# Row numbers of a group written behind the gates of the same group

## The chip, the cores and the metric

The kernel runs on one core of a Trainium2 chip. Its time is the device time of one execution in microseconds, from the first to the last instruction and the little around them. The kernel before was run three times (2207.92, 2194.14 and 2196.41 us, median 2196.41) and once more under the hardware profiler (2205.68 us, of which the span of its instructions is 2203.8 us). In what follows PE is TensorE, DVE is VectorE, ACT is ScalarE, POOL is GpSimd and SP is SyncE; PEld is the loading of weights into TensorE.

## The reference

Two stages follow one another. The first is an attention without softmax, for 8 batches of 2496 tokens with 256 channels; the second sends each of the 19968 resulting rows through one of 8 experts.

```python
scores = z @ z.T / S                       # per batch, z is 2496 x 64
x = u * (maximum(scores, 0) ** 2 @ v)      # 2496 x 256 per batch
logits = normed(x) @ normed(expert_emb).T / tau
e = argmax(logits); gate = softmax(logits)[e]
out = gate * (maximum(x @ w1[e], 0) @ w2[e])   # 256 -> 1024 -> 256
```

## The kernel before

**Attention.** Each batch is cut into five groups of tokens (four of 512, the last of 448) and twenty slices of 128 keys. For a step (batch, group, slice) PE forms the scores of the slice against the group (L266, L267), ACT takes relu and square out of PSUM (L269, L270), DVE splits the result into a high and a low float16 part (L290, L291), and PE multiplies both parts with the split values into the accumulators of the group (L329, L331, L333). Scores are symmetric, so a block above the diagonal is turned by a DMA transpose on SP's queue (L297, L299) instead of being computed again. Steps whose slices were made by an earlier group ask nothing of ACT and DVE; the last group of a batch consists of little else.

**Routing.** When the twenty steps of a group are done, the function `route` deals out its work in nineteen pieces, one per step of the next group: `gate_x` multiplies the accumulators by u (L361, tile xt), `turn` brings the result into token order with PE (L367, L368), `square`, `root` and `scale` give the norm (L374, L617 to L631, L387 to L396), `splits` writes x as two float16 halves into the tile `row` (L404 on ACT, L405 on DVE), `top` picks the expert (L415 to L427, tile ob), `gates` writes the gate weight (L441) and the row number of each token (L443) into the same tile `row`, `rank` counts the tokens of each expert on PE (L450, L451, from ob), `place` makes the target rows (L460 to L468) and `scatters` sends the four pieces of `row` into the DRAM table xs with four indirect DMAs on POOL's queue (L474). POOL clears the end of each row (L444) and the tile ob (L426).

**Slots of row.** The tile `row` comes from a pool with two buffers. So the row of a group takes the buffer of the group two before it, and whoever writes it first waits until the four scatters of that older group have landed.

**Experts.** The rows of xs are read back in tiles and multiplied with the split weights (L878 to L880 up, L902 to L904 down), and each result is scattered to its place in the output (L909). This stage begins about 1360 us into the span.

**What sets the order.** PE's order is the order in which the program is written. DVE, ACT, POOL and, up to the experts, SP are ordered by a scheduler that knows what an instruction reads and writes and has its own estimate of durations. It may put an instruction far ahead of its neighbours in the program when its inputs are there. `tc.issue_after(x)` puts the instructions of its block behind `x` in the order of their engine; it adds no wait. Each engine works through its queue in order: an instruction that waits holds back all that is queued behind it.

The row numbers (L443) read only a constant. In the kernel before, the scheduler puts the L443 of a group into DVE's queue while the group before it is at its `root`, about one group ahead of the rest of its `gates`.

Of the kernel before, what the change touches and what calls it, by code (L numbers as in the profile page):

```python
# [14 lines left out]
ALU = mybir.AluOpType  # L15
# [16 lines left out]
def ceil_div(a, b):  # L32
    return -(-a // b)
# [11 lines left out]
def relu2_attention_then_moe(ctx, tc, zT, uT, v, emb, tau, w1, w2, ident, tri, iota_e, out):  # L45
    nc = tc.nc
    B, D, S = uT.shape
# [293 lines left out]
    def route(b, g, acc, ut):  # L341

        t0, n = groups[g]
        nj = ceil_div(n, P)
        eps, oinv = scan[b, "out"]
# [8 lines left out]
        row = rt.tile([P, 4, ROW], F32, name="row", tag="row")  # L354
        rowi = row.bitcast(I32)
        row16 = row.bitcast(F16)
        loc = {}
# [78 lines left out]
        def gates():  # L436
            sm = rt.tile([P, 4], F32, name="sm", tag="sm")
            nc.vector.tensor_reduce(sm[:, :nj], loc["ex"][:, :nj, :], axis=AX.X, op=ALU.add)
            nc.vector.tensor_scalar_add(sm[:, :nj], sm[:, :nj], 1e-9)
            nc.vector.reciprocal(sm[:, :nj], sm[:, :nj])  # L440
            nc.vector.scalar_tensor_tensor(row[:, :nj, D:D + 1], sm[:, :nj].unsqueeze(2), oinv,  # L441
                                           loc["dn"][:, :nj].unsqueeze(2), op0=ALU.mult, op1=ALU.mult)
            nc.vector.tensor_scalar_add(rowi[:, :nj, D + 1:D + 2], idb[:, :nj].unsqueeze(2), float(b * S + t0))  # L443
            nc.gpsimd.memset(row[:, :, D + 2:], 0.0)  # L444

        def rank():
# [43 lines left out]
        def sq(j):  # L490
# [3 lines left out]
        return [gate_x, lambda: None, turn(0), both(turn(1), take(0)), both(take(1), sq(0)), both(turn(2), sq(1)),  # L494
                both(turn(3), take(2)), both(take(3), sq(2)), sq(3), root, scale, top, exps, splits(0),
                splits(2), gates, rank, place, scatters]


# [473 lines left out]
    for i, (b, g, q, s) in enumerate(steps):  # L972
# [16 lines left out]
        if i == 6:  # L989
# [7 lines left out]
            idb = iot[:, 4 * E:4 * E + 4]  # L997
# [156 lines left out]
```

## Time and profile before

| | |
|---|---|
| three runs | 2194.14, 2196.41, 2207.92 us, median 2196.41 |
| the profiled execution | 2205.68 us, span 2203.8 us |
| PE, PEld | busy 97% and 64% of the span |
| DVE, ACT, POOL | busy 60%, 49%, 16% |
| PE's mean granted clock | 0.991 |
| attention with routing | from about 22 us to about 1360 us |
| experts | about 1360 us to the end |

The profile is read from the top: the busy shares say which engine could be the bound, the table of stretches says in which stage it has idle time left, the lists of waits say who ended that idle time, and the order in time shows one case of it. A matmul's busy time is longer than the distance to the next one, since they overlap in the array: a 128x512 matmul is shown with 0.38 us, and the next one starts 0.22 us later.

### The profile page before, as it was taken

The page shows a single profiled execution, that of the slowest core. Times are in us where ns is not written, and L with a number is a line of the kernel's source. Part 1 is how long each engine was busy: PE and PEld are TensorE (multiplying, and loading weights), DVE is VectorE, ACT ScalarE, POOL GpSimd, SP SyncE. Part 2 cuts the span into 40 slices and gives each one's busy share as a digit, 9 for nine tenths or more (in the row PEclk, how much of TensorE's full clock was granted, in tenths as well). Part 3 has the DMA queues.
Part 4 walks back from the last instruction along what each step waited for, and adds up shares of the span by engine and source line. Part 5 has one row for each costly group of instructions (what it writes and reads, how often), then busy time and mean ns, then how long its engine had stood idle before and what let it go on. Part 6 is the DMA issues. An engine that isn't in the chain of part 4 may idle for free. (4 is left out here: it accounts for less than half of the span.)

```text
span 2203.8 us, 41437 instructions
## 1 busy us (share of the span) xinstructions
PE 2141.8 (97%) x14634; PEld 1409.9 (64%) x14634; DVE 1313.1 (60%) x3821; ACT 1080.1 (49%) x2283; POOL 346.0 (16%) x428
## 2 busy tenths in 40 slices
PE   6999999999999999999999999999999999999999
PEld 2444444445445445454455456888888888888898
DVE  7777777768767877876777755433333333333333
ACT  7667666657648757666757654222222222222221
POOL 0011111111111112111011111221111111111111
PEclk9999999999999999999999999999999999999999
DMA  7958867776866957866765853434233332237485
GB/s 196 210 105 211 171 145 180 164 190 154 201 143 162 212 129 201 164 177 167 153 172 124 178 111 94 119 88 93 68 68 92 92 88 49 57 107 203 122 218 117
DMA packets 552724, 313.85 MB, mean 142 GB/s; under 512 B 475189, under 2 KB 513086, under 8 KB 544320
## 3 DMA queue, kind: packets, MB, share of 16 engines
q1 hardware_dynamic: 537040, 269.53, 53.7%
q0 software_dynamic: 15184, 41.24, 5.9%
q8 instruction: 117, 1.92, 0.4%
q14 instruction: 95, 0.78, 0.1%
q10 hardware_dynamic: 288, 0.39, 0.1%
HBM read 272.94 MB, written 59.60 MB: 151 GB/s over the span
## 5 line engine op out<-in xcount | busy, mean ns | idle before, releaser
L269 ACT ACTIVATE a<-sc 128x512 f32<-128x512 f32 (+1 forms) x480 | 268.2, 559 | 157.0 <-PE sc L267 99.2
L270 ACT ACTIVATE a<-a 128x512 f32<-128x512 f32 (+1 forms) x480 | 286.3, 597 | 11.7
L333 PEld LDWEIGHTS <-vv 128*128 128x128 f16 x1600 | 157.4, 98 | 188.4 <-issue 12.6
L329 PEld LDWEIGHTS <-vv 128*128 128x128 f16 x1600 | 157.2, 98 | 161.6 <-issue 3.8
L331 PEld LDWEIGHTS <-vv 128*128 128x128 f16 x1520 | 149.5, 98 | 168.9 <-issue 20.1
L909 POOL DMA_INDIRECT out_dram<-ot,me x159 | 154.6, 973 | 653.8 <-DVE ot L908 618.8
L904 PE MATMUL po<-w,hl 128*128 128x256 f16 x928 | 253.0, 273 | 0.0
L903 PE MATMUL po<-w,hh 128*128 128x256 f16 x928 | 253.0, 273 | 0.0
L902 PE MATMUL po<-w,hh 128*128 128x256 f16 x928 | 252.9, 273 | 0.0
L474 POOL DMA_INDIRECT xs<-row,dsti x160 | 172.7, 1079 | 419.9 <-DMA xs<-row,dsti 361.9
L329 PE MATMUL acc<-tt,vv 128*128 128x512 f16 (+1 forms) x640 | 236.4, 369 | 0.0
L331 PE MATMUL acc<-tt,vv 128*128 128x512 f16 (+1 forms) x640 | 236.3, 369 | 0.0
L908 DVE TENSOR_SCALAR ot<-po,me,w 128x256 f32<-128x256 f32 x116 | 58.2, 539 | 219.2 <-PE po L904 216.6
L333 PE MATMUL acc<-tt,vv 128*128 128x512 f16 (+1 forms) x640 | 184.0, 369 | 0.0
L266 PE MATMUL sc<-z 128*128 128x512 f16 (+1 forms) x480 | 177.0, 369 | 3.1 <-DVE z L189 3.1
L267 PE MATMUL sc<-z,z 128*128 128x512 f16 (+1 forms) x480 | 177.0, 369 | 0.0
L903 PEld LDWEIGHTS <-hh 128*128 128x128 f16 x1272 | 124.5, 98 | 14.8 <-issue 0.6
L904 PEld LDWEIGHTS <-hl 128*128 128x128 f16 x1272 | 124.5, 98 | 14.4
L902 PEld LDWEIGHTS <-hh 128*128 128x128 f16 x1272 | 124.5, 98 | 14.2
L378 ACT COPY x<-pt 128x264 f32<-128x264 f32 x160 | 59.9, 374 | 140.5 <-PE pt L368 136.6
L902 PE MATMUL po<-wb,hh 128*128 128x256 f16 x344 | 93.8, 273 | 0.5 <-DMA wb<-wsd 0.5
L904 PE MATMUL po<-wb,hl 128*128 128x256 f16 x344 | 93.8, 273 | 0.0
(3881 smaller groups left out, 4942.5 us busy)
## 6 DMA issues: line engine op xcount, KB each, us to landing
w<-wsd SPq DMA_DIRECT2D x64, 1026.0 KB
wa<-wsd SPq DMA_DIRECT2D x46, 1024.0 KB
w<-wsd SPq DMA_DIRECT2D x42, 1024.0 KB
wb<-wsd SPq DMA_DIRECT2D x24, 1026.0 KB
vt<-in_v_dram SPq DMA_DIRECT2D x140, 128.0 KB
scan<-in_v_dram SPq DMA_DIRECT2D x56, 320.0 KB
ut<-in_uT_dram SPq DMA_DIRECT2D x32, 512.0 KB
wr<-in_w_dram SPq DMA_DIRECT2D x16, 1024.0 KB
```

The source lines that it names most:

```text
L266: nc.tensor.matmul(sc[:, :n], z1[:, ss], z1[:, t0:t0 + n], start=True, stop=False)
L267: nc.tensor.matmul(sc[:, :n], z1[:, ss], z2[:, t0:t0 + n], start=False, stop=True)
L269: state["at"] = nc.scalar.activation(a[:, :n], sc[:, :n], AF.Relu, scale=2.0 ** -SHIFT).ins
L270: nc.scalar.activation(a[:, :n], a[:, :n], AF.Square)
L329: nc.tensor.matmul(o, va, ph, start=first, stop=False)
L331: nc.tensor.matmul(o, vb, ph, start=False, stop=False)
L333: nc.tensor.matmul(o, vb if last else va, pl, start=False, stop=ends)
L474: put = nc.gpsimd.indirect_dma_start(xs[:, :], bass.IndirectOffsetOnAxis(ap=loc["dsti"][:m, j:j + 1], axis=0), row[:m, j, :], None)
L902: nc.tensor.matmul(o, hh[:, f, t], wh, start=(f == 0), stop=False)
L903: nc.tensor.matmul(o, hh[:, f, t], wl, start=False, stop=False)
L904: nc.tensor.matmul(o, hl[:, f, t], wh, start=False, stop=(f == NF - 1))
L909: put = nc.gpsimd.indirect_dma_start(out, bass.IndirectOffsetOnAxis(ap=me.bitcast(U32)[:, j, 1:2], axis=0), ot[:, j, :], None, bounds_chec ...
```

## The change

The instruction that writes the row numbers is put behind the instruction that writes the gate weights of the same group. Nothing is added or removed; what is computed is the same.

```diff
-            nc.vector.scalar_tensor_tensor(row[:, :nj, D:D + 1], sm[:, :nj].unsqueeze(2), oinv,
-                                           loc["dn"][:, :nj].unsqueeze(2), op0=ALU.mult, op1=ALU.mult)
-            nc.vector.tensor_scalar_add(rowi[:, :nj, D + 1:D + 2], idb[:, :nj].unsqueeze(2), float(b * S + t0))
+            gw = nc.vector.scalar_tensor_tensor(row[:, :nj, D:D + 1], sm[:, :nj].unsqueeze(2), oinv,
+                                                loc["dn"][:, :nj].unsqueeze(2), op0=ALU.mult, op1=ALU.mult).ins
+            with tc.issue_after(gw):
+                nc.vector.tensor_scalar_add(rowi[:, :nj, D + 1:D + 2], idb[:, :nj].unsqueeze(2), float(b * S + t0))
             nc.gpsimd.memset(row[:, :, D + 2:], 0.0)
```

Every line number from L443 on is one higher in the changed kernel: the row numbers are L444 there. The queues of PE, ACT and POOL, with POOL's clearings of ob and of the end of row, hold the same instructions in the same order in both kernels. On DVE the row numbers move in all 40 groups.

DVE's queue in the last group of the second batch, while the fourth group of that batch is routed. `row_4008` is the row of the group being routed, `row_4373` that of the last group, whose own routing comes after. Before:

```order
L392 TENSOR_SCALAR dn_4198<-h23_4194 128x4
L624 TENSOR_TENSOR xt_4163<-xy_4161 128x4
L626 SCALAR_TENSOR_TENSOR xt2_4165<-xt_4163,xn2c_4157 128x4
L443 TENSOR_SCALAR row_4373<-iot_222 128x4
L239 SCALAR_TENSOR_TENSOR vv_4133<-vt_4067,scv_3628,vv_4133 128x256
L628 SCALAR_TENSOR_TENSOR xy_4167<-xt2_4165,xy_4161 128x4
L405 SCALAR_TENSOR_TENSOR row_4008<-x_4005,up_4196,row_4008 128x256
```

The same place in the changed kernel:

```order
L392 TENSOR_SCALAR dn_4198<-h23_4194 128x4
L625 TENSOR_TENSOR xt_4163<-xy_4161 128x4
L627 SCALAR_TENSOR_TENSOR xt2_4165<-xt_4163,xn2c_4157 128x4
L239 SCALAR_TENSOR_TENSOR vv_4133<-vt_4067,scv_3628,vv_4133 128x256
L629 SCALAR_TENSOR_TENSOR xy_4167<-xt2_4165,xy_4161 128x4
L405 SCALAR_TENSOR_TENSOR row_4008<-x_4005,up_4196,row_4008 128x256
```

The write into `row_4373` has gone from between the steps of the square root of the older group.

DVE's queue one group later in the changed kernel, at the gates of `row_4373`:

```order
L439 TENSOR_SCALAR sm_4717<-sm_4717 128x4
L291 TENSOR_TENSOR hl__4701<-a_4667,hl__4701 128x4x128
L440 RECIPROCAL sm_4717<-sm_4717 128x4
L441 SCALAR_TENSOR_TENSOR row_4373<-sm_4717,cinv_1573,dn_4604 128x4
L444 TENSOR_SCALAR row_4373<-iot_222 128x4
L290 CAST hl__4724<-a_4688 128x4x128
```

The row numbers now stand directly behind the gate weights; in all 40 groups at most one or two instructions lie between them. Before them in the queue are the four splits (L405) of the same row, which DVE begins after ACT's L404; both L404 and the first L405 wait for the same four scatters for which L443 waited before.

The scheduler also arranges a few neighbours anew, most at two places, in the second and in the sixth batch. DVE's queue at the first of them, where the scan of the next batch's values (L114) stands beside `gate_x` (L361). Before:

```order
L290 CAST hl__3204<-a 128x4x128
L523 TENSOR_REDUCE wm<-pm 2x1
L291 TENSOR_TENSOR hl__3204<-a,hl__3204 128x4x128
L524 TENSOR_SCALAR wm<-wm 2x1
L114 TENSOR_REDUCE smxv<-scan 128x1
L526 TENSOR_SCALAR wmb<-wm 2x1
L361 TENSOR_TENSOR xt<-acc_2770,ut 128x512
L528 TENSOR_SCALAR dg<-idt,wmb 2x2
L361 TENSOR_TENSOR xt<-acc_2771,ut 128x512
```

The same place in the changed kernel:

```order
L524 TENSOR_REDUCE wm<-pm 2x1
L290 CAST hl__3204<-a 128x4x128
L525 TENSOR_SCALAR wm<-wm 2x1
L114 TENSOR_REDUCE smxv<-scan 128x1
L527 TENSOR_SCALAR wmb<-wm 2x1
L291 TENSOR_TENSOR hl__3204<-a,hl__3204 128x4x128
L529 TENSOR_SCALAR dg<-idt,wmb 2x2
L361 TENSOR_TENSOR xt<-acc_2770,ut 128x512
L361 TENSOR_TENSOR xt<-acc_2771,ut 128x512
```

The low part of `hl__3204` now stands behind the scan's reduction and ahead of `gate_x`. On SP's queue at these two places one load of the scan stands ahead of two transposes (L299) instead of behind them, and at two other places a load of z stands behind one more load of v.

## Rows read from the trace of the kernel before

**Rows 1.** Stretches start, attention, experts: length, busy of each engine, PEclk, DMA.

```profile
0.00:30.00 30.00, 11.57 (x29) 4.30 (x30) 20.81 (x56) 16.34 (x32) 1.08 (x10) 0.83 0.68 212
30.00:1360.00 1330.00, 1294.98 (x6564) 653.30 (x6563) 980.56 (x3186) 870.08 (x1918) 184.46 (x252) 0.99 0.71 163
1360.00:2204.00 844.00, 835.27 (x8044) 752.29 (x8042) 311.73 (x580) 193.69 (x335) 160.44 (x166) 1.00 0.43 108
```

**Rows 2.** Line L443: its instructions; idle time before them (us, times) by releaser.

```profile
L443 DVE TENSOR_SCALAR row<-iot x40: 150/172/199, 22.0 to 1343.9; 128x4 int32<-128x4 f32 x40
...
  DMA xs<-row,dsti: 50.3, 16
```

**Rows 3.** PE's waits from 30 to 1360 us: total, times, longest.

```profile
PE pm L450 <- DVE ob L427: 13.5, 4, 4.9
...
PE acc L329 <- DVE hl__7500 L290: 3.5, 1, 3.5
...
PE acc L329 <- DVE hl__5438 L290: 1.6, 1, 1.6
...
PE acc L329 <- DVE hl__3380 L290: 0.4, 1, 0.4
PE acc L333 <- DVE hl__5438 L291: 0.4, 1, 0.4
```

**Rows 4.** DVE in order of time: start, us, instruction, [idle before, releaser].

```profile
350.79 0.17 DVE L443 TENSOR_SCALAR row<-iot 128x4 int32<-128x4 f32 x1 [6.01 <-DMA xs<-row,dsti]
...
355.97 0.48 DVE L239 SCALAR_TENSOR_TENSOR vv<-vt,scv,vv 128x256 f16<-128x256 f32 x1
...
356.81 0.19 DVE L427 TENSOR_TENSOR ob<-iot,m 128x32 bf16<-128x32 f32 x1
```

**Rows 5.** PE in order of time, at the place of rows 4.

```profile
357.05 0.27 PE L450 MATMUL pm<-ob,ones_b 128*128 128x40 bf16 x4 [3.99 <-DVE ob L427]
```

**Rows 6.** Stretches right after PE's four longest gaps, columns as in rows 1.

```profile
187.00:190.00 3.00, 3.00 (x14) 1.24 (x13) 2.84 (x11) 2.09 (x5) 0.16 (x1) 0.51 0.69 189
...
357.00:360.50 3.50, 3.45 (x14) 1.47 (x15) 3.26 (x13) 2.55 (x6) 0.16 (x1) 0.53 0.47 133
...
625.00:630.00 5.00, 5.00 (x13) 1.81 (x12) 4.72 (x18) 3.48 (x7) 0.00 (x0) 0.50 0.50 96
...
1028.00:1033.00 5.00, 5.00 (x14) 1.96 (x13) 3.39 (x11) 3.27 (x7) 1.30 (x2) 0.50 0.47 141
```

**Rows 7.** DVE in order of time: the wait for the row split at 344.54.

```profile
318.33 0.17 DVE L443 TENSOR_SCALAR row<-iot 128x4 int32<-128x4 f32 x1 [2.77 <-DMA xs<-row,dsti]
```

**Rows 8.** ACT in order of time, at the place of rows 4.

```profile
344.54 0.91 ACT L404 ACTIVATE row<-x,up 128x256 f16<-128x256 f32 x2 [0.37 <-issue]
...
350.03 0.51 ACT L238 ACTIVATE vv<-vt,scv 128x256 f16<-128x256 f32 x1 [1.02 <-DMA vt<-in_v_dram]
```

**Rows 9.** DVE in order of time: seven waits at L443; start, us, instruction, [idle before, releaser].

```profile
180.70 0.17 DVE L443 TENSOR_SCALAR row<-iot 128x4 int32<-128x4 f32 x1 [3.87 <-DMA xs<-row,dsti]
...
281.23 0.17 DVE L443 TENSOR_SCALAR row<-iot 128x4 int32<-128x4 f32 x1 [2.62 <-DMA xs<-row,dsti]
...
453.25 0.17 DVE L443 TENSOR_SCALAR row<-iot 128x4 int32<-128x4 f32 x1 [3.17 <-DMA xs<-row,dsti]
...
621.49 0.17 DVE L443 TENSOR_SCALAR row<-iot 128x4 int32<-128x4 f32 x1 [6.65 <-DMA xs<-row,dsti]
...
751.24 0.17 DVE L443 TENSOR_SCALAR row<-iot 128x4 int32<-128x4 f32 x1 [2.78 <-DMA xs<-row,dsti]
...
854.51 0.17 DVE L443 TENSOR_SCALAR row<-iot 128x4 int32<-128x4 f32 x1 [1.89 <-DMA xs<-row,dsti]
...
1021.39 0.17 DVE L443 TENSOR_SCALAR row<-iot 128x4 int32<-128x4 f32 x1 [8.00 <-DMA xs<-row,dsti]
```

**Rows 10.** DVE in order of time, beside gate_x in the second batch.

```profile
265.27 0.67 DVE L291 TENSOR_TENSOR hl__3204<-a,hl__3204 128x512 f16<-128x512 f32 x1
...
267.40 0.82 DVE L114 TENSOR_REDUCE smxv<-scan 128x1 f32<-128x640 f32 x1 [1.40 <-DMA scan<-in_v_dram]
```

**Rows 11.** PE in order of time, 24 us after a wait at L443.

```profile
775.54 0.50 PE L367 MATMUL pt<-rhs,xt 128*128 128x136 f32 x2 [1.85 <-DVE xt L361]
```

**Rows 12.** Tile row: the scatters, ns min/median/max, first and last start.

```profile
L474 POOL DMA_INDIRECT xs<-row,dsti x160: 898/965/2771, 94.4 to 1408.3; - x160
```

## The prediction

> **What bounds the kernel now.** I read the page first, then the stretches, then the waits of one line and of one engine, and last one case in order of time. There PE is shown busy for 97% of the span. By stretches it is idle for 1330.00 - 1294.98 = 35.0 us in the attention and for 8.7 us in the experts [rows 1]; the change touches the attention alone. The attention is therefore PE's, and what another engine does counts only where PE stands still for it. The reader should see next that DVE stands still at L443, the row numbers, 50.3 us in 16 of 40 cases, always for the scatters of an older row [rows 2]. The instruction itself takes 0.17 us. It needs nothing that a computation makes: it waits because its buffer is the one of two that the group before last is still being scattered from.
>
> The list of PE's waits says what this costs [rows 3]: 13.5 us in four cases where the count of the experts (L450) waits for DVE's ob, and single cases where the values wait for a split (hl). One case in order of time shows the chain [rows 4, 5]. DVE stands at L443 for 6.01 us until 350.79 and then works without a pause to ob at 356.81. PE has run out of work at 353.06 (357.05 - 3.99) and stands 3.99 us until L450 starts. The wait is longer than the gap it makes, as PE had some work in hand.
>
> There is a second cost that busy time hides. After the four longest gaps (three at L450, one at hl__7500) PE is shown as busy nearly throughout, but at a granted clock of 0.50 to 0.53 [rows 6]: that is its lower level, 1.2 instead of 2.4 GHz, and the work takes twice as long. The Trainium skill, Perfetto Trace Analysis, section Identifying the Most-Contended Engine, says that matmul busy share does not measure how close a kernel is to its limit. The rows agree: 3.00 of 3.00 us busy at clock 0.51. By busy time alone the gain below would be 19.4 us; with the clock it is 27.5 us.
>
> **The change, part by part.**
>
> *The wait at L443.* The instruction moves behind the gates of its own group, in all 40 groups. The scatters for which it waited are also waited for by the first split of the same row, on ACT (L404) and now on DVE (L405). So the question is whether they have landed by then. The narrowest case among the sixteen is this: the wait ended at 318.33 [rows 7], the splits of that row began at 344.54 [rows 8], 26.2 us later. L404 had to wait for the same landings before the change as well; the first is shown with 0.37 us of issue and no DMA. I take the new wait at 0; it could cost something only if landings slipped by over 26 us.
>
> *PE's idle time.* I follow the sixteen waits to PE. Seven reach it within some 10 us. Those of 3.87, 6.01, 1.89 and 8.00 us make the four gaps at L450, 13.5 us; one of 6.65 us the 3.5 at hl__7500; one of 3.17 us the 1.6 + 0.4 at hl__5438; one of 2.62 us the 0.4 at hl__3380 [rows 3, 4, 9]. Sum 13.5 + 3.5 + 1.6 + 0.4 + 0.4 = 19.4 us. Each wait is longer than the gap behind it (8.00 against 4.9, the longest), so without it the gap should close.
>
> What is late next? In the case shown, ACT's split of a value (L238) stands until 350.03 for its load and ends at 350.54 [rows 8]. DVE's half of it (L239) is shown at 355.97, and from its start to the end of ob (356.81 + 0.19) pass 1.03 us [rows 4]. So ob could be there by 351.6 at the earliest, where PE wants it at 353.06: 1.5 us to spare. I count the gap as closed.
>
> *PE's clock.* The lost time is length times (1 - clock) [rows 6]: 3.0 x 0.49 + 3.5 x 0.47 + 5.0 x 0.50 + 5.0 x 0.50 = 8.1 us. Without the four gaps it is not lost. Waits and clock together: 27.5 us.
>
> *The two rearranged places.* There hl's low part (0.67 us) comes ahead of gate_x instead of ahead of the scan's reduction, which stands waiting for its load until 267.40 [rows 10]. Gate_x starts up to 0.67 us later, and PE's turn waits for it: at most 2 x 0.67 = 1.3 us lost. I take it whole. The load that passes two transposes on SP and the two loads of z behind a load of v are 2 DMAs and 2 DMAs in other places of a queue; their tiles are read a group or several steps later, so 0.
>
> *A possible extra.* At 775.54 PE waits 1.85 us for gate_x [rows 11], 24 us after the wait of 2.78 us [rows 9]. If this lateness is left over from that wait, 1.85 us more will go; but DVE last stood there for a load of the scan, so I take 0 and keep 1.85 for the range.
>
> *The instruction itself.* 40 x 0.17 us stay on DVE, at another place, beside PE's work: 0. If they lay bare, 6.8 us.
>
> **Sum.** -27.5 + 1.3 = -26.2 us. Against the profiled execution's own 2205.7 us this is 2179.5. That execution is 9.3 us above the median of 2196.4, and the runs spread over 13.8 us. If the spread comes from these very waits, which depend on when DMAs land, the changed kernel should be near 2179.5 in each run; if it comes from elsewhere, the median falls to 2170.2. I have no row that decides it and take the middle, 2174.8, rounded towards the median's side: **2174 us**.
>
> **Rivals.**
>
> *The gaps come back in part.* The 1.5 us that ob has to spare hang on one load of v; where a load lands later than here, PE's gap comes back with another cause. For it: ACT already stands for that load. Against it: the gaps are shorter than their waits. If half the 26.2 us returns: 2205.7 - 13.1 = 2192.6 from the profile, 2183.3 from the median.
>
> *Nothing comes of it.* The wait moves to the split or to a load and PE stands as long as before, 2196 us. That the change does not do what it says can be left out: the order shows the move 40 times. Against this rival speaks the distance of 26.2 us.
>
> *More than I count.* All of PE's 35.0 us of idle time in the attention is due to DVE's lateness [rows 1], with 8.1 us of clock: 2196.4 - 43.1 = 2153. Against it: there are gaps with no wait at L443 in the 20 us ahead of them.
>
> *Slower.* DVE's idle time was also quiet time for POOL, which issues the scatters. If the four scatters of a row get so much later that they have not landed at the splits, ACT waits at L404, and ACT also takes the scores out of PSUM; then both engines stand and PE with them. The point from which this decides is a slip of 26.2 us per row. To be over 1% slower it has to give back 26.2 us and cost 22 us more, 48 us over 40 groups, or 1.2 us in each: a slip of some 27.4 us. A scatter took 0.898 us at least and 2.771 at most on POOL [rows 12]; four of them at the worst are 4 x 1.87 = 7.5 us later. So: 2220 us or more, but hardly reached. The Trainium skill, SBUF — State Buffer, section SBUF: two separate sides, says that some DVE operations lock POOL out of a port that they share, so that it cannot write the descriptors of its DMAs. By that rule more work on DVE makes scatters later, as in this rival; no row here shows by how much.
>
> **How the numbers follow.** About 1% is what a measurement of this kernel can tell from no change; 1% below the median is 2174.4 us, beside my forecast. Chances: the forecast (2166 to 2181) 0.70, of which 0.40 below 2174.4, since the change is measured against a median that lay lower than the profiled execution; more than I count 0.06; gaps back in part 0.13; nothing 0.06; slower 0.05. Faster by over 1%: 0.40 + 0.06 = 0.46. Within 1%: 0.30 + 0.13 + 0.06 = 0.49. Slower: 0.05. The range reaches down to the fastest run less the gain and the extra, 2194.1 - 27.5 - 1.9 = 2164.7, rounded to 2164, and up to the first rival from the profiled execution, 2193. That leaves out most of the large gain, of nothing and of slower: under 0.2.
>
> **What would show it.** At L443's successor, L444, no idle time for a DMA, where 50.3 us stood. At L404 and L405 none either. L450 waiting for ob: 13.5 us gone or under 2. The granted clock in the attention without stretches of 0.5 after 150 us. PE's idle time in the attention down from 35.0 to about 16 us, and the stretch shorter by 26 us, the experts unchanged at 844 us. The forecast is wrong if DVE shows the same idle time under another line, with loads of v or of the scan or ACT's work as releasers, or if waits of L404 for the scatters appear.

## The result, and the profile after

| | before | after |
|---|---|---|
| median of the runs | 2199.84 us (4 runs, 2194.14 to 2207.92) | 2173.13 us (4 runs, 2171.66 to 2174.66) |
| ratio, 95% interval | | 0.9876 [0.9840, 0.9912] |
| profiled execution, span | 2205.68, 2203.8 us | 2171.66, 2169.9 us |
| PE's mean granted clock | 0.991 | 0.999 |

The kernel is 1.24% faster. The changed kernel was timed once more beside the experiments: 2173.81 us against 2204.65, ratio 0.9868 [0.9844, 0.9892]. One execution of the kernel with the moved scan took 8247 us, beside five others near 2162, and is left out.

The stretches of the profile after, as in [rows 1] (the attention ends about 30 us earlier, so its stretch is cut there). PEclk in the first row can't be compared: it is shown as 1.00 although matmuls of 128x512 start 0.43 us apart until 27 us, twice the 0.22 us of full clock.

```profile
0.00:30.00 30.00, 11.72 (x35) 4.69 (x36) 20.97 (x56) 16.67 (x33) 1.08 (x10) 1.00 0.68 212
30.00:1330.00 1300.00, 1282.48 (x6578) 652.00 (x6576) 986.21 (x3187) 873.34 (x1921) 184.95 (x252) 1.00 0.73 167
1330.00:2170.00 840.00, 833.07 (x8026) 750.40 (x8023) 310.75 (x579) 192.37 (x330) 160.43 (x166) 1.00 0.43 107
```

PE is idle 1300.00 - 1282.48 = 17.5 us in the attention, where it was 35.0. Where the experts begin is shown by the first weight load of their first product, the first of the two start times. In the kernel before:

```profile
L878 PEld LDWEIGHTS <-wa x736: 95/98/98, 1357.8 to 2182.4; 128*128 128x128 f16 x184
```

and after:

```profile
L879 PEld LDWEIGHTS <-wa x736: 95/98/98, 1325.1 to 2149.0; 128*128 128x128 f16 x184
```

The attention is 32.7 us shorter; from that load to the end of the span it was 846.0 us and is now 844.8. The row numbers themselves, the answer to [rows 2]:

```profile
L444 DVE TENSOR_SCALAR row<-iot x40: 155/165/339, 90.9 to 1345.1; 128x4 int32<-128x4 f32 x40
```

No row of idle time follows it: the 50.3 us are gone. Did they move to the first writer of `row`? The instructions of L404 on ACT, and what ended the idle time before them:

```profile
L404 ACT ACTIVATE row<-x,up x160: 491/494/509, 76.8 to 1340.7; 128x256 f16<-128x256 f32 x160
...
  issue: 11.1, 16
```

There is no DMA among the releasers (issue was 11.7 us in 18 cases before), and at L405 on DVE there is none either. The longest of PE's waits from 30 to 1330 us, the answer to [rows 3]:

```profile
PE pt L367 <- DVE xt L361: 7.3, 8, 1.5
PE acc L329 <- DVE hl__15416 L290: 2.8, 1, 2.8
...
PE acc L329 <- DVE hl__7135 L290: 1.0, 1, 1.0
```

The count of the experts (L451 now) no longer waits for `ob`, and the waits for hl__7500, hl__5438 and hl__3380 have left the list. At the place of [rows 4, 5] DVE now shows

```profile
344.36 0.19 DVE L427 TENSOR_TENSOR ob<-iot,m 128x32 bf16<-128x32 f32 x1
344.81 0.17 DVE L444 TENSOR_SCALAR row<-iot 128x4 int32<-128x4 f32 x1
```

and PE

```profile
346.06 0.26 PE L451 MATMUL pm<-ob,ones_b 128*128 128x40 bf16 x4
```

`ob` is ready at 344.55, 1.5 us before PE asks for it. The stretches where half clock stood in [rows 6], and the only one left in the attention:

```profile
1230.00:1232.00 2.00, 2.00 (x12) 1.01 (x11) 1.93 (x5) 0.41 (x1) 0.00 (x0) 0.50 1.03 192
345.00:360.00 15.00, 15.00 (x83) 7.88 (x82) 13.21 (x29) 12.06 (x25) 4.07 (x6) 1.00 0.63 162
186.00:190.00 4.00, 4.00 (x22) 1.99 (x21) 3.93 (x8) 3.29 (x7) 1.67 (x2) 1.00 0.62 237
622.00:631.00 9.00, 9.00 (x51) 5.40 (x50) 8.37 (x23) 4.58 (x15) 1.57 (x2) 1.00 0.64 163
```

At one and the same place, the first products behind the count in the first batch (tile hl__1921), matmuls now start 0.19 us apart, where they started 0.37 us apart before at clock 0.51, with the same full busy share. Before:

```profile
188.11 0.58 PE L331 MATMUL acc<-hl__1921,vv 128*128 128x448 f16 x1
188.48 0.58 PE L329 MATMUL acc<-hl__1921,vv 128*128 128x448 f16 x1
```

and after:

```profile
184.20 0.35 PE L329 MATMUL acc<-hl__1921,vv 128*128 128x448 f16 x1
184.39 0.35 PE L331 MATMUL acc<-hl__1921,vv 128*128 128x448 f16 x1
```

I read the granted clock of the whole attention in stretches of 2 us and summed length times (1 - clock) where it was under 0.98: 13.7 us before, 1.7 us after.

### The profile page after: what moved, and what is told of

It is laid out like the page before. It is cut to its first block, busy times and chain, and to the rows that moved or that the text cites. A ratio compares the mean times of both kernels' runs of the same rounds, so it can differ in the third digit from the quotient of the medians.

```text
span 2169.9 us, 41478 instructions
## 1 busy us (share of the span) xinstructions
PE 2127.3 (98%) x14634; PEld 1407.1 (65%) x14634; DVE 1317.9 (61%) x3821; ACT 1082.4 (50%) x2283; POOL 346.5 (16%) x428
## 5 line engine op out<-in xcount | busy, mean ns | idle before, releaser
L270 ACT ACTIVATE a<-a 128x512 f32<-128x512 f32 (+1 forms) x480 | 286.3, 596 | 11.7
L475 POOL DMA_INDIRECT xs<-row,dsti x160 | 173.0, 1081 | 411.7 <-DMA xs<-row,dsti 355.0
L905 PEld LDWEIGHTS <-hl 128*128 128x128 f16 x1272 | 124.5, 98 | 14.4
```

Of the source, the lines that this page charges most:

```text
L270: nc.scalar.activation(a[:, :n], a[:, :n], AF.Square)
L475: put = nc.gpsimd.indirect_dma_start(xs[:, :], bass.IndirectOffsetOnAxis(ap=loc["dsti"][:m, j:j + 1], axis=0), row[:m, j, :], None)
L905: nc.tensor.matmul(o, hl[:, f, t], wh, start=False, stop=(f == NF - 1))
```

## The experiments

The theory: DVE stood at the head of its queue because the early row numbers claimed a buffer of `row` a whole group before it was needed; PE's gaps and the half clock behind them follow from that. Each kernel was timed against the kernel before on the same chip. Two chips were used, so experiments are compared with each other by their ratios.

**The wait put back.** The row numbers stay behind the gates, but one column of POOL's clearing of the tile becomes a small write on DVE, which the scheduler again puts one group ahead.

```diff
-            nc.gpsimd.memset(row[:, :, D + 2:], 0.0)
+            nc.vector.memset(row[:, :nj, D + 2:D + 3], 0.0)
+            nc.gpsimd.memset(row[:, :, D + 3:], 0.0)
```

> The kernel after, with one added write to the row tile on DVE (a memset of its third column) that stands, in DVE's order, where the row numbers of the kernel before stood, one group ahead; the row numbers themselves stay behind the gates. Theory (the kernel before lost its time because DVE waited at the head of its queue for the scatters of the row two groups older): the memset now waits about 50 us in about 16 of 40 cases, the waits of L450 for the output tile come back with about 13.5 us of PE idle time, and the time is that of before, 2190 to 2205 us, ratio to before 0.995 to 1.005. Rival (what counted was where the row numbers themselves and the two clearings stand): no change against the kernel after, 2171 to 2176 us, ratio 0.988.

Measured: 2215.05 us, ratio 1.0051 [1.0031, 1.0070]. The waits of DVE, and of PE:

```profile
DVE row L445 <- POOL row L446: 44.7, 13, 8.8
```

```profile
PE pm L452 <- DVE ob L427: 17.7, 4, 5.8
```

The wait and the gaps are back, though the row numbers stand where the change put them, so the rival falls as far as it goes by their place. The time overshot my range by 10 us. One case in order of time shows how the wait reaches DVE here, first POOL and then DVE:

```profile
182.20 0.10 POOL L446 MEMSET row<- 128x4 f32 x1 [4.28 <-DMA xs<-row,dsti]
```

```profile
182.31 0.06 DVE L445 MEMSET row<- 128x4 f32 x1 [3.97 <-POOL row L446]
```

POOL's clearing waits for the scatters, and DVE for POOL. So two things moved here, and not one: in the kernel after, POOL's clearing stands behind the splits, and here it too has gone a group ahead, with 101.3 us of waiting for the scatters in 38 cases. That part of the rival is left to the kernel with one buffer, below, where the clearing stands behind the splits and the wait is back all the same. The gaps at the count are 4.2 us longer than the 13.5 of [rows 3], the clock costs 17.0 us instead of 13.7, and the two rearranged places stay. Why the four gaps grew although the waits are shorter in sum was not settled.

**The last group of each batch alone.** Eight of forty groups.

```diff
-            with tc.issue_after(gw):
+            with ExitStack() as behind:
+                if g == NG - 1:
+                    behind.enter_context(tc.issue_after(gw))
```

> The row numbers stand behind the gates in the last group of each batch alone (8 of 40 groups), and as before in the other 32; the two places where hl and the gates' work changed their order are as in the kernel before. Theory: the four longest waits (3.87, 6.01, 1.89 and 8.00 us, 19.8 of the 50.3 us) go, with 13.5 us of PE idle time at L450 and 5.6 us of half clock behind three of the gaps: minus 19 us, about 2180 us, ratio 0.991; the row numbers still idle about 30 us in about 12 cases. Rival (each group gives the same, or the rearrangement gives it): 8/40 of 26.7 us = minus 5 us or nothing, 2194 to 2200 us, ratio 0.998 to 1.

Measured: 2185.35 us, ratio 0.9916 [0.9893, 0.9939], by the ratio -18.5 us of 2204.12. The count's wait is gone from PE's list. Of DVE's wait this is left, as forecast:

```profile
DVE row L446 <- DMA xs<-row,dsti: 30.4, 12, 5.3
```

In this profile the gaps left at hl__5438 and hl__7500 (2.59 and 2.19 us) had no half clock behind them, so part of the 18.5 us may be the clock of other groups' gaps.

**The other 32 groups alone.** As above with `g < NG - 1`.

> The reverse of the kernel with the last groups: the row numbers stand behind the gates in the 32 other groups and as before in the last of each batch; the two rearranged places are as in the kernel after. Theory: it gets 5.9 us of PE idle time (3.5, 1.6, 0.4, 0.4) and 2.5 us of half clock, up to 3 us more at 775 us, and pays 1 to 2 us at the rearranged places: minus 6 to minus 9 us, about 2191 us, ratio 0.996; the four waits of L450 for the output tile stay, about 13.5 us. Rival (each group gives the same): 32/40 of 26.7 us = minus 21 us, about 2178 us, ratio 0.990.

Measured: 2193.70 us, ratio 0.9964 [0.9933, 0.9994], or -7.9 us. What is left of the waits of PE, and of DVE:

```profile
PE pm L453 <- DVE ob L427: 12.9, 4, 4.5
```

```profile
DVE row L446 <- DMA xs<-row,dsti: 21.6, 5, 7.6
```

So 21.6 us of DVE's wait in five cases are worth more, about twice as much by the middles of the two intervals, than 30.4 us in twelve. The two parts add up: -18.5 - 7.9 = -26.4 us, against 0.0124 x 2199.84 = -27.3 us for the whole change; each part is known to 5 to 7 us. A wait of DVE has no price of its own; it has the price of the gap that it makes at PE, and all four gaps at the count stand in last groups.

**The row numbers on GpSimd.** One edit of the kernel before; they stay early.

```diff
-            nc.vector.tensor_scalar_add(rowi[:, :nj, D + 1:D + 2], idb[:, :nj].unsqueeze(2), float(b * S + t0))
+            nc.gpsimd.tensor_scalar_add(rowi[:, :nj, D + 1:D + 2], idb[:, :nj].unsqueeze(2), float(b * S + t0))
```

> The kernel before with one edit: the row numbers are written by GpSimd and not by DVE, early in its queue, one group ahead. Theory (what costs is that DVE stands, whichever engine else has to wait is cheap, since GpSimd issues the scatters itself and nothing in PE's path waits for it in that time): the 50 us of waiting stand on GpSimd, the L450 waits of 13.5 us are gone, and the time is 2168 to 2176 us, ratio 0.987 to 0.990. Rival (the wait only moves: GpSimd's clearing of the next output tile is late behind it, and L450 waits for that as before): the time of before, 2192 to 2203 us, ratio 0.997 to 1.002.

Measured: 2170.98 us, ratio 0.9844 [0.9827, 0.9860]. POOL's wait:

```profile
POOL row L443 <- DMA xs<-row,dsti: 125.1, 37, 6.4
```

The wait is there, 125.1 us long, PE no longer waits for `ob`, and the time is that of the kernel after or a little below: the wait costs nothing that shows, as it stands on an engine that PE does not depend on at that time. So it is not the early place as such, nor the order of gates and row numbers, but the engine that stands.

**One buffer for row.** The kernel after with the slack taken away.

```diff
-        row = rt.tile([P, 4, ROW], F32, name="row", tag="row")
+        row = rt.tile([P, 4, ROW], F32, name="row", tag="row", bufs=1)
```

> The kernel after with one buffer for the row tile instead of two: the splits at L404 (ACT) and L405 (DVE) must now wait for the scatters of the group just before, the wait that the prediction's rival on the slower side turns on. Theory (the scatters of a row land some 26 us ahead of the first split with two buffers, and a group is about 30 us long, so one buffer uses the slack up): waits of 2 to 8 us at L404 in many of 40 groups, the gaps of PE are back, 2195 to 2230 us, ratio 0.998 to 1.014. Rival (landings come early enough even for one buffer): no wait at L404, 2171 to 2176 us, ratio 0.986 to 0.989.

Measured: 2204.53 us against 2204.65, ratio 0.9998 [0.9979, 1.0018]. ACT's wait at L404 in sum, PE's wait for `ob`, and two cases of ACT's:

```profile
ACT row L404 <- DMA xs<-row,dsti: 50.0, 13, 8.6
```

```profile
PE pm L451 <- DVE ob L427: 14.4, 4, 5.1
```

```profile
345.98 0.91 ACT L404 ACTIVATE row<-x,up 128x256 f16<-128x256 f32 x2 [8.48 <-DMA xs<-row,dsti]
...
1022.09 0.91 ACT L404 ACTIVATE row<-x,up 128x256 f16<-128x256 f32 x2 [8.55 <-DMA xs<-row,dsti]
```

The gain is gone, to within the 4 us of the interval: 50.0 us of waiting stand for 50.3 in [rows 2], and PE's wait for `ob` is 14.4 us for 13.5 in [rows 3]. The kernel before waited for the same landings, at nearly the same places (350.79 and 1021.39, [rows 4, 9]): although it had two buffers, its early L443 made them worth one. The prediction's slower rival has its mechanism here, a wait at L404 that ACT, DVE and PE pay for; it decides once the slack is one group shorter than the change leaves it. A third buffer was not tried.

**The scan moved.** What PE still waits for in the kernel after is L361, which stands behind the scan's maxima (L114). DVE there:

```profile
261.94 0.82 DVE L114 TENSOR_REDUCE smxv<-scan 128x1 f32<-128x640 f32 x1 [2.26 <-DMA scan<-in_v_dram]
...
262.74 0.67 DVE L291 TENSOR_TENSOR hl__3204<-a,hl__3204 128x512 f16<-128x512 f32 x1
...
263.46 1.27 DVE L361 TENSOR_TENSOR xt<-acc,ut 128x512 f32<-128x512 f32 x2
```

This experiment moves that scan work 6 steps back, on the kernel after:

```diff
-            todo.append((at + 2 * i, False, lambda w=what: scan_load(b + 1, *w)))
-            todo.append((at + 2 * i + 4, False, lambda w=what: scan_max(b + 1, *w)))
+            due = at + 2 * i
+            if due + 4 > 2 * NST - 3:
+                due += 6
+            todo.append((due, False, lambda w=what: scan_load(b + 1, *w)))
+            todo.append((due + 4, False, lambda w=what: scan_max(b + 1, *w)))
```

> The kernel after, with those scan loads and scan maxima of the next batch that would fall beside the gates of its first four tiles put 6 steps later; no operation is added or left out. Theory (the last repeated gap of PE, about 7 us in 8 waits of L367 for L361, stands because the scan's maxima at L114, which wait for their DMA, are ahead of gate_x in DVE's queue): the waits shrink to under 2 us and the time falls by 4 to 8 us against the kernel after, to about 2166 us, ratio to before 0.983 to 0.985. Rival (L361 is late for its own x transfer or for ACT, or the maxima stall something else where they land): no change, 2170 to 2175 us.

Measured: 2161.69 us, ratio 0.9812 [0.9792, 0.9832]; 12 us less than the kernel after on the same chip, more than I expected. Run again for its profile:

> The kernel with the scan work put 6 steps later once more, for a profile. By its other runs it takes 2161 to 2163 us, 12 us less than the kernel after, where its waits of L367 for L361 (7.1 us in 8 cases) were thought to be worth 4 to 8 us. Theory (those waits explain it: each is followed by some time more, at L368 or at half clock, and the clearance behind the accumulators of eight batches goes with them): the eight waits are gone or under 2 us together, and the excess of PE's intervals falls by 10 to 12 us from the 41 of the kernel after. Rival (something else became shorter): the excess falls by under 7 us, and the rest lies in the first or the last stretch.

Measured: 2161.88 us, ratio 0.9812 [0.9781, 0.9843]. PE's waits and the attention's stretch:

```profile
PE pt L367 <- DVE xt L361: 1.7, 2, 1.3
PE acc L329 <- DVE hl__15416 L290: 1.7, 1, 1.7
```

```profile
30.00:1320.00 1290.00, 1277.51 (x6569) 650.98 (x6568) 983.08 (x3188) 874.78 (x1921) 184.04 (x252) 1.00 0.73 168
```

The waits at L367 fell from 7.1 us in eight cases to 1.7 in two, and PE's idle time from 17.2 (in the second profile of the kernel after) to 12.5 us. The one gap in front of half clock shrank from 3.2 to 1.7 us and the clock stayed full, which gives 1.7 us more. By the distances of PE's starts the excess over each kind's median distance fell by 7.3 us, between my two bounds, while the profiled spans differ by 9.1 us. The experts begin 9.1 us earlier as well (1325.1 to 1316.0), and the first 30 us give only 0.3, so the rival's place for the rest, the first or the last stretch, falls. The mechanism holds for about 7 us. Some 2 us of the profile I can't place, and the other 3 of the 12 lie between the profiled execution of the kernel after (2171.21 us) and its median (2173.81).

**Both.** GpSimd's row numbers and the moved scan, on the kernel before.

> Both together on the kernel before: the row numbers written by GpSimd, and the scan work put 6 steps later as in the kernel with the moved scan. Theory (the two waits are apart, so the gains add): the time of the kernel with GpSimd's row numbers less what the moved scan gives, 2162 to 2168 us, ratio to before 0.980 to 0.983. Rival (the moved scan gives nothing): 2168 to 2173 us, ratio 0.984 to 0.987.

Measured: 2163.11 us, ratio 0.9814 [0.9792, 0.9836]: no better than the moved scan on the kernel after. The 2.8 us between the medians of GpSimd's kernel and the kernel after, taken on two chips, don't add to it. Of them 0.8 us can be the two rearranged places, where PE stands 1.6 us with GpSimd's row numbers and 2.4 in the kernel after, and which the moved scan clears in either kernel; the rest was not placed.

**The moved scan alone.** The same edit on the kernel before.

> The kernel before with the moved scan alone; the row numbers are where they were. Theory (the two waits are independent): the gain of the moved scan is the same as on the kernel after, 12 us, 2190 to 2194 us, ratio to before 0.993 to 0.996, and DVE still idles some 50 us at L443. Rival (the moved scan pays only where L443 is out of the way, since DVE's lateness from L443 fills its place): 2198 to 2206 us, ratio 0.998 to 1.001.

Measured: 2201.62 us, ratio 0.9996 [0.9979, 1.0014]. My theory of independent waits falls. DVE's wait, and PE's waits:

```profile
DVE row L443 <- DMA xs<-row,dsti: 59.5, 20, 7.4
```

```profile
PE pm L450 <- DVE ob L427: 11.7, 4, 4.3
PE acc L329 <- DVE hl__5436 L290: 2.9, 1, 2.9
PE acc L329 <- DVE hl__9583 L290: 2.6, 1, 2.6
...
PE pt L367 <- DVE xt L361: 1.7, 2, 0.9
```

L361's waits are gone as in the kernel after, but L443's grew by 9.2 us, in 20 cases instead of 16, and new gaps stand at the values. I read this as DVE reaching L443 earlier while the scatters land no earlier; that the landings stayed was not shown one by one. The edit is worth 12 us behind the change and nothing clear of the interval, 4 us each way, ahead of it.

The kernel after with the moved scan and the one with both edits are the fastest, 1.9% under the kernel before; between the two the runs do not decide.

## Why the prediction was right, step by step

The forecast of 2174 us stands 0.9 us from the median. Not every term was that good: two misses cancelled, and that the number came this close is luck. The mechanism, from DVE's wait to PE's gaps and clock, was right.

- **DVE's wait goes, and no wait replaces it.** Right: no DMA at L444, L404 or L405. The distance of 26.2 us [rows 7, 8] was enough; with one buffer instead of two, ACT stood up to 8.6 us, which shows that the slack is real and less than a group.
- **PE's idle time, -19.4 us, and the 1.5 us to spare.** The gaps behind the seven waits are gone, and `ob` came 1.5 us ahead of PE's request. With the cost of the rearranged places I had -18.1 us; measured -17.5.
- **The rearranged places, at most 1.3 us.** Nearly right in size. PE's waits for gate_x at the two places before:

```profile
268.92 0.50 PE L367 MATMUL pt<-rhs,xt 128*128 128x136 f32 x2 [0.44 <-DVE xt L361]
269.65 0.50 PE L368 MATMUL pt<-rhs,xt 128*128 128x136 f32 x2 [0.23 <-DVE xt L361]
...
941.34 0.50 PE L368 MATMUL pt<-rhs,xt 128*128 128x136 f32 x2 [0.23 <-DVE xt L361]
```

After, at both places:

```profile
264.19 0.50 PE L367 MATMUL pt<-rhs,xt 128*128 128x136 f32 x2 [1.42 <-DVE xt L361]
...
914.20 0.50 PE L367 MATMUL pt<-rhs,xt 128*128 128x136 f32 x2 [0.99 <-DVE xt L361]
```

PE's wait at L368 is gone there, so 2.41 - 0.90 = 1.5 us; in the second profile of the kernel after it is 2.09 - 0.90 = 1.2. I counted hl's low part, 0.67 us, but not that DVE may stand longer for the scan's load ahead of it: 2.26 us instead of 1.40 [rows 10] at the first place.
- **The possible extra, taken at 0.** It came in part: the wait of 1.85 us [rows 11] is 0.69 after. Behind it half clock had cost 1.7 us more, which I had not looked at.
- **PE's clock, -8.1 us.** The mis-sized term: -12.0 us measured (13.7 to 1.7). The four stretches of [rows 6] were cut to their flat parts; read in steps of 2 us with their edges they are 10.3 us, and the place of the extra adds 1.7. The mechanism was right: without these gaps the clock stays up. The sign that I named, no stretch of 0.5 after 150 us, was not met: the one behind the wait for hl__15416 stands in both kernels (2.3 us of waiting before, 2.8 after, with the wait at L443 gone), and I had not seen it.
- **The sum against the profiled execution.** 2179.5 us forecast, 2171.7 measured. The 7.8 us between them are 3.9 of the clock, less 0.6 of idle time, 1.2 in the experts, and 3.2 more ahead of the experts. Of these, 1.2 us lie at the start, where nothing has waited at L443 yet (the first such wait ends at 111.43). The same matmul before and after:

```profile
30.22 0.38 PE L329 MATMUL acc<-hl__263,vv 128*128 128x512 f16 x1
```

```profile
29.01 0.38 PE L329 MATMUL acc<-hl__263,vv 128*128 128x512 f16 x1
```

PE's matmuls came to their full pace earlier there; in the other profiles this matmul starts between 28.65 and 30.17 us, with the early wait and without it, so I take this part as chance and not as the change. The other 2.0 us are open. For 1.0 of them there is an estimate: a gap is counted from the shown end of a matmul, 0.16 us behind the place where the next would have started (0.38 less 0.22), and the list of PE's waits has 25 cases before and 19 after.
- **Profile or median.** I took the middle between 2179.5 and 2170.2 because I had no row on where the runs' spread came from. The runs of the kernel after spread over 3.0 us, those of before over 13.8; the kernels here that still wait at the head of a queue in PE's path spread over 7.8 to 14.8 us, the one with the wait on GpSimd over 1.7 and the one with both edits over 5.7. So the spread goes with these waits, which does not show that they make all of it; by my own argument I should have kept to the profiled execution: 2179.5. The step to the middle made up for the clock that was missing from the sum.
- **The rivals.** "Nothing" and "gaps back in part" fell. "More than I count" was right in its direction for the clock alone; 17.5 us of idle time stay. The slower one did not occur: a scatter took 965 ns of POOL in the median before [rows 12] and 962 after, and the wait of one scatter for the landing of the one before it was 361.9 us in 116 cases and is 355.0 in 117, so with DVE's fuller use they came no slower. The rule that I cited from the Trainium skill, SBUF — State Buffer, section SBUF: two separate sides, speaks of some DVE operations that hold a port which POOL needs; the change adds no operation to DVE, and these times show no effect of it.

## What to carry to other kernels

Look for instructions that read only constants and write a buffer from a pool: a scheduler may put them far ahead, as it did here, and there they take the buffer's wait to the head of an in-order queue. Price such a wait by the gap that it makes on the bound engine, and by the granted clock behind the gap, not by its own length; and cut no edges off a stretch of half clock. A second edit that shows nothing may only be masked: the moved scan was worth nothing that showed with the wait in place and 12 us without it. And what a gap costs in clock is not fixed by its length, so one profile gives one case of it.

## What the runs showed of the hardware that was not expected

The half clock cost two thirds as much as the idle time itself: 12.0 us beside a net 17.5 went with the same few gaps. In the profiles before and after it followed each gap of PE, in the attention, from the 1.85 us at 775.54 [rows 11] to the 4.9 us at the count [rows 3], and not the wait of 1.6 us for hl__5438. But the length of a gap does not settle it. With the last groups alone the clock fell behind a gap of 1.57 us (the products start 0.43 us apart behind it) and not behind those of 2.59 and 2.19:

```profile
761.08 0.50 PE L367 MATMUL pt<-rhs,xt 128*128 128x136 f32 x2 [1.57 <-DVE xt L361]
...
762.19 0.63 PE L329 MATMUL acc<-tt,vv 128*128 128x512 f16 x1
762.62 0.63 PE L331 MATMUL acc<-tt,vv 128*128 128x512 f16 x1
```

With the other 32 groups alone it stayed up behind a gap of 3.50 us (0.22 us apart):

```profile
1246.49 0.38 PE L329 MATMUL acc<-hl__15416,vv 128*128 128x512 f16 x1 [3.50 <-DVE hl__15416 L290]
1246.71 0.38 PE L331 MATMUL acc<-hl__15416,vv 128*128 128x512 f16 x1
```

So the 12.0 us belong to these two profiles, and what one gap costs in clock can't be read off its length. In the kernel with the moved scan, where the longest gap is 1.7 us, the clock stays at its upper level through the attention.
